# Block-causal attention and a gated MLP on one core: the MLP in 9 chunks of 512 tokens instead of 16 halves of 288

## The chip, the cores and the metric

The kernel runs on one core of one Trainium2 chip. The metric is device microseconds for one execution; the median of three runs of the kernel before is 1021.64 us (1021.4 to 1022.11). A profile of one execution of the kernel before is shown as well. PE is the matrix engine, PEld its weight loads, DVE, ACT and POOL are the vector, scalar and GpSimd engines, SP is the engine that issues most of the transfers.

## The reference

Attention over 8 batches, 8 heads, 576 tokens and 64 channels a head, where a token sees its own block of 64 and all earlier blocks. Its output, brought to tokens by 512 channels, goes through a gated MLP without a nonlinearity.

```python
scores = scale * np.matmul(q, k.transpose(0, 1, 3, 2))      # scale = 1/8
scores = np.where(block_i >= block_j, scores, -1e9)
attn = softmax(scores)                                       # max taken off, sum + 1e-09
x = np.matmul(attn, v) -> (8 * 576 tokens, 8 * 64 channels)
a = x @ w1                                                   # 512 x 1024
b = x @ w2                                                   # 512 x 1024
h = a * b @ w3                                               # 1024 x 1024
out = h @ w_out                                              # 1024 x 512
```

The kernel multiplies w3 by w_out once and keeps the product as `wh`, `wl`. There are 4608 tokens in all: 8 batches of 576, or 9 times 512.

## The kernel before

**Number format.** A factor is held as two parts, a rounded one (`..h`, `hi`) and the remainder (`..l`, `lo`), both in the matmul type `fp32r`; a product takes three matmuls, high by high, low by high, high by low. ACT or DVE writes the high part, POOL mostly the low one.

**Attention.** The work goes by pairs of heads, n = 0 to 31, four pairs to a batch. `load(n)` brings q, k and v of a pair in one transfer of 896 KB (128 partitions x 1792 numbers) into one of two buffers `raw`. For each of the two heads j of a pair, `prep_qk` makes `hi[j]` (the rounded q and k), two transfers that copy halves of it (`hi<-hi`, `lo<-hi`), and two POOL subtractions of 64x576 numbers for the remainders. `shift_mask` computes a bound of each block's row maximum with cheap matmuls, and two small transfers `lo<-ms`, one for each head, put it into a row of `lo[j]`. `prep_v` splits v into `vs` with one ACT cast and one POOL subtraction. `s_tile` then makes scores `s` in five steps S0 to S4 a head (widths 288, 288, 448, 320, 192+64), the exponentials `p` and `ph` on ACT, the remainder `pl` on DVE and the running row sum `rsum` on POOL. `pv` multiplies `ph`, `pl` by `vs` in five steps c = 0 to 4 into `x`. The first four pairs (n < 4) use plain fp32 and run while the weights are decoded.

**x.** `take` adds the two halves of `x` in PSUM into `x32`, `norm` divides by the row sum, and `finish_x` splits the pair's 576 tokens at once into two halves of 288: ACT casts `xh`, POOL subtracts `xl`. 12 such buffers of each kind exist, so the MLP of a batch reads them while the next batch's are filled.

**MLP.** `gen_moe(b)` handles a batch as two halves of 288 tokens. For each of 8 steps f it makes two sums `ab` of 12 matmuls of 288 columns; then ACT copies one (`a32`), DVE multiplies (`g32`), ACT casts `gh`, POOL subtracts `gl`. For each of 4 steps e it makes one sum `o` of 24 matmuls, which ACT copies (`o32`) and SP writes out as `out_t` (144 KB). A `yield` stands after every 6 matmuls, and such a piece is the unit of interleaving.

**What sets the order.** The table `PLAN` (one row for each head of a pair) is a list of letters: S a score step, V a pv step, B and A the prepare steps of this pair's second and the next pair's first head, M a step of the mask, Q `prep_v` of the next pair and, in the second head, `load(n + 2)`, R, N, T the sums, `take` and `norm`, and F one MLP piece. There are 24 F in the two rows, so 24 pieces a pair, 28 pairs long. From pair 4 on PE executes exactly the written order. The other engines' queues are put in order by a scheduler that works with due times. What the interleaved pieces don't cover runs at the end, with no attention beside it.

**Queues.** All transfers but those of the first pairs are issued by SP, one after the other; an issue that waits for a buffer holds those behind it. A buffer `raw` comes free for `load(n + 2)` when its last reader is done, which is the POOL subtraction of `prep_v` (`vs<-raw`). The scheduler moves loads up: `load(17)`, written in pair 15, is issued at the end of pair 14.

## Time and profile before

| what | value |
|---|---|
| median of 3 runs | 1021.64 us |
| profiled execution: span from first to last instruction | 1019.4 us |
| what lies around the span, by the median | 2.2 us |
| mean granted TensorE clock | 0.982 |
| PE busy | 965.8 us (95%) |
| DVE, ACT, POOL busy | 744.7, 547.4, 596.6 us |

The profiled execution's own device time is not listed beside its span; the span is compared with the median of the runs, which lie within 0.7 us. Three stages are seen. In the first 160 us four pairs run in plain fp32 while the weights are loaded and decoded. From about 170 to 940 us the 28 other pairs run, some 27.5 us each, with MLP pieces between their steps. From 943 to 1016.2 us only the MLP is left. Matmul records carry a duration longer than their pitch, since they overlap; so the time that a matmul costs is read from the distance between starts.

In rows of the profile a form such as `128x288` is partitions by elements, and `[0.29 <-ACT ph L252]` says how long the engine idled before the instruction and what ended it.

### The profile page before, as it was taken

The numbers are of one execution on the slowest core, as the hardware profiler recorded it, in microseconds if no ns is written. First come the engines' busy times: TensorE is split into PE (matmuls) and PEld (weight loads), VectorE is DVE, ScalarE is ACT, GpSimd is POOL, SyncE is SP. The second block draws the span as 40 slices with busy tenths as digits, with TensorE's granted clock in tenths as the row PEclk, the third lists the DMA queues.
The fourth block names the chain that finished last, engine by engine and source line by source line (L and its number), as shares of the span: only waits on it lengthen the run. The fifth ranks groups of instructions, "written<-read, shape, count | busy, mean of one in ns | idle before, by whom it ended". The sixth has DMA issues, their size and how long they took to land.

```text
span 1019.4 us, 18475 instructions
## 1 busy us (share of the span) xinstructions
PE 965.8 (95%) x6594; PEld 888.3 (87%) x6624; DVE 744.7 (73%) x1320; ACT 547.4 (54%) x1433; POOL 596.6 (59%) x625
## 2 busy tenths in 40 slices
PE   3878878999999999999999999999999999999998
PEld 1444346999999999999999999999999999999998
DVE  7899886777787777777777778777777777775100
ACT  3645555656555555555565655555555556553221
POOL 3242466667676666767576767666675757673211
PEclk9889897999999999999999999999999999999999
DMA  8566542122212222222212221222222221110000
GB/s 299 170 205 196 172 122 59 49 83 61 61 51 69 73 60 73 66 78 61 84 49 84 61 66 46 70 72 64 69 67 78 60 85 48 48 25 25 1 24 24
DMA packets 37436, 80.42 MB, mean 79 GB/s; under 512 B 5408, under 2 KB 21920, under 8 KB 37344
## 3 DMA queue, kind: packets, MB, share of 16 engines
q1 hardware_dynamic: 35564, 76.26, 24.5%
q10 hardware_dynamic: 1780, 2.97, 1.2%
q8 instruction: 52, 0.85, 0.4%
q14 instruction: 40, 0.33, 0.1%
HBM read 50.76 MB, written 9.44 MB: 59 GB/s over the span
## 4 chain that ended last, share of the span: by engine, by line
PE 67%; DVE 16%; ACT 8%; issue 4%; DMA 4%; SPq 0%; ACTq 0%; POOL 0%; DVEq 0%; POOLq 0%
PE ab L387 28%; PE o L403 20%; PE s L236 7%; PE x L291 6%; DVE pl L254 5%; PE mx L183 3%; ACT ph L252 2%; ACT p L251 2%; DVE g L394 2%; PE x L275 1%; DVE wbits L138 1%; DMA wraw<-in_w 1%; DMA wraw<-in_w3t 1%; DVE wbits L136 1%; DVE x L329 1%
## 5 line engine op out<-in xcount | busy, mean ns | idle before, releaser
L257 POOL TENSOR_TENSOR rsum<-rsum,p 128x448 f32<-128x448 f32 x224 | 176.7, 789 | 108.4 <-ACT p L251 98.6
L254 DVE TENSOR_TENSOR pl<-p,ph 128x448 fp32r<-128x448 f32 x168 | 148.3, 896 | 60.1 <-ACT ph L252 59.2
L396 POOL TENSOR_TENSOR gl<-g,gh 128x288 fp32r<-128x288 f32 x128 | 107.5, 840 | 120.1 <-ACT gh L395 118.7
L395 ACT CAST gh<-g 128x288 fp32r<-128x288 f32 x128 | 55.5, 433 | 217.1 <-DVE g L394 217.1
L387 PE MATMUL ab<-xh,w2h 128*128 128x288 f32 x512 | 154.4, 301 | 0.0
L403 PE MATMUL o<-gh,wh 128*128 128x288 f32 x512 | 153.7, 300 | 0.0
L387 PE MATMUL ab<-xh,w1h 128*128 128x288 f32 x512 | 151.7, 296 | 1.6 <-ACT xh L338 1.6
L387 PE MATMUL ab<-xl,w2h 128*128 128x288 f32 x512 | 151.8, 296 | 0.0
L387 PE MATMUL ab<-xl,w1h 128*128 128x288 f32 x512 | 151.4, 296 | 0.3 <-POOL xl L339 0.3
L387 PE MATMUL ab<-xh,w2l 128*128 128x288 f32 x512 | 151.7, 296 | 0.0
L387 PE MATMUL ab<-xh,w1l 128*128 128x288 f32 x512 | 151.4, 296 | 0.0
L403 PE MATMUL o<-gl,wh 128*128 128x288 f32 x512 | 151.1, 295 | 0.0
L403 PE MATMUL o<-gh,wl 128*128 128x288 f32 x512 | 151.0, 295 | 0.0
L187 DVE TENSOR_REDUCE m<-mx 128x1 f32<-128x512 f32 (+6 forms) x320 | 128.7, 449 | 19.3 <-PE mx L183 17.4
L252 ACT ACTIVATE ph<-s 128x288 fp32r<-128x288 f32 x336 | 131.3, 393 | 0.8 <-issue 0.8
L236 PE MATMUL s<-hi 128*128 128x288 f32 (+4 forms) x384 | 123.0, 332 | 6.8 <-ACT pe L244 4.0
L211 POOL TENSOR_TENSOR hi<-raw,hi 64x576 fp32r<-64x576 f32 x64 | 92.9, 1451 | 33.3 <-ACT hi L157 16.4
L254 DVE TENSOR_TENSOR pl<-rsum,ph 128x288 fp32r<-128x288 f32 x112 | 74.6, 685 | 49.0 <-ACT ph L252 48.8
L251 ACT ACTIVATE p<-s 128x448 f32<-128x448 f32 x224 | 85.4, 381 | 46.3 <-PE s L236 43.3
L236 PE MATMUL s<-lo 128*128 128x288 f32 (+4 forms) x384 | 106.8, 306 | 3.4 <-issue 2.5
L394 DVE TENSOR_TENSOR g<-ab,a 128x288 f32<-128x288 f32 x128 | 57.7, 451 | 71.3 <-PE ab L387 63.3
L291 PE MATMUL x<-ph,vs 128*128 128x128 f32 x336 | 104.2, 320 | 0.0
(73 smaller groups left out, 2418.1 us busy)
## 6 DMA issues: line engine op xcount, KB each, us to landing
raw<-in_qkv SPq DMA_DIRECT2D x32, 896.0 KB
out_t<-o SPq DMA_DIRECT2D x64, 144.0 KB
wraw<-in_w3t SPq DMA_DIRECT2D x16, 512.0 KB
wraw<-in_w SPq DMA_DIRECT2D x16, 512.0 KB
hi<-hi SPq DMA_DIRECT2D x54, 144.0 KB
lo<-hi SPq DMA_DIRECT2D x54, 144.0 KB
wraw<-in_wout SPq DMA_DIRECT2D x8, 512.0 KB
hi<-hi ACTq DMA_DIRECT2D x10, 144.0 KB
```

What stands on the lines that cost most here:

```text
L187: nc.vector.reduce_max(m[:, col : col + 1], sc, axis=AX.X)
L211: nc.gpsimd.tensor_tensor(out=hi[j][x, 1, :], in0=rqk[o, 1, :], in1=hi[j][o, 1, :], op=ALU.subtract)
L236: nc.tensor.matmul(t[ks, at : at + q1 - q0], src[:, 1, kr], src[:, 0, q0:q1], start=(s == 0), stop=(s == 1))
L251: nc.scalar.activation(p32, t[ks, at : at + w], AF.Exp, scale=SCALE)
L252: nc.scalar.activation(ph[ks, o : o + w], t[ks, at : at + w], AF.Exp, scale=SCALE)
L254: nc.vector.tensor_tensor(out=low, in0=p32, in1=ph[ks, o : o + w], op=ALU.subtract)
L257: nc.gpsimd.tensor_tensor(out=r, in0=r, in1=p32, op=ALU.add)
L291: nc.tensor.matmul(xps[:, to : to + w], v[:, c, :], pr[:, a : a + w], start=(u < 2 and s == 0), stop=(u in (0, len(PV) - 1) and s == len(p ...
L387: nc.tensor.matmul(t[:, 0:HALF], l[:, c, fs], r, start=(c == 0 and s == 0), stop=(c == NC - 1 and s == 2))
L394: nc.vector.tensor_tensor(out=g32, in0=acc[1][:, 0:HALF], in1=a32, op=ALU.mult)
L396: nc.gpsimd.tensor_tensor(out=gl[:, f, :], in0=g32, in1=gh[:, f, :], op=ALU.subtract)
L403: nc.tensor.matmul(t[:, 0:HALF], l[:, f, es], r[:, f, :], start=(f == 0 and s == 0), stop=(f == NF - 1 and s == 2))
```

## The change

**Tokens.** The MLP goes over all 4608 tokens in 9 chunks of 512 (`gen_moe(i)`, i = 0 to 8), so a chunk may span two batches. A matmul, an `ab` or `o` sum and the ACT, DVE and POOL instructions behind it have 512 columns. There are 9 x (192 + 96) = 2592 MLP matmuls instead of 16 x 288 = 4608. A piece is now 3 matmuls. The plan is unchanged, with 24 F a pair; the first 7 chunks are interleaved, and the last two run at the end.

**x.** `take` and `norm` work in `ring`, four fp32 buffers of 1024 tokens; a batch of 576 tokens that crosses the ring's end is written in two pieces (batches 1, 3, 5 and 7). `finish_x` is gone. In its place `split_x(i, c)` makes one buffer `xh[c]`, `xl[c]` of 512 tokens just before its chunk: three of a chunk's four splits are written behind the o steps 0 to 2 of the chunk before, the fourth at the chunk's start. For chunk 0 all four stand at its start.

**Buffers.** `a32` and `o32` share one buffer, `g32` has one, where each had two. `kb` shares a buffer with `rb`.

**Loads.** q and k of a pair (128x1152, 576 KB) and v (128x640, 320 KB) come in two transfers. `raw` still has two buffers, `rawv` has one.

What the diff doesn't show is where these instructions come to stand. On SP, at the end of pair 14, before (`raw17` is the load of pair 17, `ms15` the mask row of pair 15; 0 and 1 behind `lo` are the heads):

```order
L209 DMA hi1_85<-hi1_85 64x576
L210 DMA lo1_87<-hi1_85 64x576
L200 DMA lo0_86<-ms15_5246 1x9x64
L200 DMA lo1_87<-ms15_5246 1x9x64
L94 DMA raw17_5592<-in_qkv 128x1792
```

and in the changed kernel at the same place:

```order
L221 DMA hi1_82<-hi1_82 64x576
L222 DMA lo1_84<-hi1_82 64x576
L98 DMA raw17_4464<-in_qkv 128x1152
L212 DMA lo0_83<-ms15_4205 1x9x64
L103 DMA rawv16_4185<-in_qkv 128x640
L212 DMA lo1_84<-ms15_4205 1x9x64
L428 DMA out_t<-o32_4237 128x512
```

The load of q and k has moved from behind the two mask rows to a place before them; the load of v stands between them, and ahead of the first at the end of pairs 20 to 23, 28 and 29, as here at the end of pair 20:

```order
L221 DMA hi1_82<-hi1_82 64x576
L222 DMA lo1_84<-hi1_82 64x576
L98 DMA raw23_6132<-in_qkv 128x1152
L103 DMA rawv22_5847<-in_qkv 128x640
L212 DMA lo0_83<-ms21_5867 1x9x64
L212 DMA lo1_84<-ms21_5867 1x9x64
```

On ACT, in the first head of pair 14, steps S3 and S4, before:

```order
L251 ACTIVATE p14_0_4956<-s14_0_4953 128x320
L252 ACTIVATE ph_1147<-s14_0_4953 128x320
L395 CAST gh_1152<-g32_4976 128x288
L251 ACTIVATE p14_0_4992<-s14_0_4987 128x192
L252 ACTIVATE ph_1147<-s14_0_4987 128x192
```

and in the changed kernel:

```order
L415 CAST gh_1127<-g32_3956 128x512
L263 ACTIVATE p14_0_3978<-s14_0_3975 128x448
L264 ACTIVATE ph_1122<-s14_0_3975 128x448
L263 ACTIVATE p14_0_3986<-s14_0_3983 128x320
L264 ACTIVATE ph_1122<-s14_0_3983 128x320
L413 COPY a32_4044<-ab_3968 128x512
L263 ACTIVATE p14_0_4006<-s14_0_4001 128x192
L264 ACTIVATE ph_1122<-s14_0_4001 128x192
```

Between the exponentials of S3 and S4 stood a cast `gh`, which follows a DVE product; there stands now a copy `a32`, which follows a PE sum, and the cast has moved ahead of S2's exponentials.

On POOL, in the second head of pair 14, before:

```order
L257 TENSOR_TENSOR rsum_1148<-rsum_1148,p14_1_5125 128x320
L257 TENSOR_TENSOR rsum_1148<-rsum_1148,p14_1_5155 128x192
L257 TENSOR_TENSOR rsum_1148<-rsum_1148,p14_1_5160 64x64
L211 TENSOR_TENSOR hi1_85<-raw15_4842,hi1_85 64x576
L213 TENSOR_TENSOR lo1_87<-raw15_4842,hi1_85 64x576
L396 TENSOR_TENSOR gl_1153<-g32_5192,gh_1152 128x288
L226 TENSOR_TENSOR vs1_1151<-raw15_4842,vs1_1151 128x5x64
```

and in the changed kernel:

```order
L269 TENSOR_TENSOR rsum_1123<-rsum_1123,p14_1_4111 128x320
L359 TENSOR_TENSOR xl0_1133<-ring0_88,xh0_1129 128x512
L359 TENSOR_TENSOR xl1_1134<-ring1_89,xh1_1130 128x512
L269 TENSOR_TENSOR rsum_1123<-rsum_1123,p14_1_4131 128x192
L269 TENSOR_TENSOR rsum_1123<-rsum_1123,p14_1_4136 64x64
L223 TENSOR_TENSOR hi1_82<-raw15_3904,hi1_82 64x576
L225 TENSOR_TENSOR lo1_84<-raw15_3904,hi1_82 64x576
L416 TENSOR_TENSOR gl_1128<-g32_4164,gh_1127 128x512
L238 TENSOR_TENSOR vs1_1126<-rawv15_3902,vs1_1126 128x5x64
```

Two subtractions `xl` of 512 columns have come in ahead of S4's row sums in this pair, which is one where a chunk ends. The last reader of `raw` is now the subtraction for `lo1`, one place ahead of `gl`; `vs1` reads `rawv`.

The diff, cut where lines only hand arguments through:

```diff
-HALF = S // 2
-RAW = 2 * S + 640
+TOK = 512
+NCHUNK = NT // TOK
+RING = 2 * TOK
+QK = 2 * S
+VW = 640
...
+    ring = [cpool.tile([P, RING], F32, name=f"ring{c}") for c in range(NC)]
...
     def load(n):
-        t = raws.tile([P, RAW], F32, tag="raw", name=f"raw{n}")
-        nc.sync.dma_start(out=t, in_=qkv[n // NPAIR, n % NPAIR])
+        t = raws.tile([P, QK], F32, tag="raw", name=f"raw{n}")
+        nc.sync.dma_start(out=t, in_=qkv[n // NPAIR, n % NPAIR][:, 0:QK])
         raw_of[n] = t
 
+    def load_v(n):
+        t = raws.tile([P, VW], F32, tag="rawv", name=f"rawv{n}", bufs=1)
+        nc.sync.dma_start(out=t, in_=qkv[n // NPAIR, n % NPAIR][:, QK : QK + VW])
+        v_of[n] = t
...
-        tl["gh"] = pool.tile([P, NF, HALF], F32R, name="gh")
-        tl["gl"] = pool.tile([P, NF, HALF], F32R, name="gl")
+        tl["gh"] = pool.tile([P, NF, TOK], F32R, name="gh")
+        tl["gl"] = pool.tile([P, NF, TOK], F32R, name="gl")
+        tl["xh"] = [pool.tile([P, TOK], F32R, name=f"xh{c}") for c in range(NC)]
+        tl["xl"] = [pool.tile([P, TOK], F32R, name=f"xl{c}") for c in range(NC)]
...
-        kb = work.tile([P, S], BF16, tag="kb", name=f"kb{n}")
+        kb = work.tile([P, S], BF16, tag="tr", name=f"kb{n}")
...
+    def pieces(n):
+        at, left, done = (n // NPAIR) * S % RING, S, 0
+        while left:
+            w = min(left, RING - at)
+            yield slice(done, done + w), slice(at, at + w)
+            done, at, left = done + w, (at + w) % RING, left - w
...
-    def take(n, j, xps, x32):
+    def take(n, j, xps):
         o, x = own[j], oth[j]
-        xl = tl["late"].tile([P, S], F32, tag="xlow", name=f"xlow{n}_{j}")
-        nc.scalar.copy(xl[o], xps[x, 384:960])
-        nc.vector.tensor_tensor(out=x32[o], in0=xps[o, 384:960], in1=xl[o], op=ALU.add)
+        for a, r in pieces(n):
+            dst = ring[n % NPAIR][o, r]
+            cols = slice(384 + a.start, 384 + a.stop)
+            nc.scalar.copy(dst, xps[x, cols])
+            nc.vector.tensor_tensor(out=dst, in0=xps[o, cols], in1=dst, op=ALU.add)
...
-        (nc.gpsimd if n < 2 else nc.vector).tensor_tensor(out=x32, in0=x32, in1=rb, op=ALU.mult)
-
-    def finish_x(n, x32):
-        for h in range(2):
-            at = (2 * n + h) % 12
-            pool, bufs = (xpool, 8) if at < 8 else (tl["late"], 4)
-            xh = pool.tile([P, HALF], F32R, tag="xh", name=f"xh{n}_{h}", bufs=bufs)
-            xl = pool.tile([P, HALF], F32R, tag="xl", name=f"xl{n}_{h}", bufs=bufs)
-            src = x32[:, h * HALF : (h + 1) * HALF]
-            nc.scalar.copy(xh, src)
-            nc.gpsimd.tensor_tensor(out=xl, in0=src, in1=xh, op=ALU.subtract)
-            x_of[n // NPAIR, n % NPAIR, h] = (xh, xl)
+        for a, r in pieces(n):
+            dst = ring[n % NPAIR][:, r]
+            (nc.gpsimd if n < 2 else nc.vector).tensor_tensor(out=dst, in0=dst, in1=rb[:, a], op=ALU.mult)
+
+    def split_x(i, c):
+        src = ring[c][:, i * TOK % RING : i * TOK % RING + TOK]
+        nc.scalar.copy(tl["xh"][c], src)
+        nc.gpsimd.tensor_tensor(out=tl["xl"][c], in0=src, in1=tl["xh"][c], op=ALU.subtract)
...
+    def gen_moe(i):
+        gh, gl = tl["gh"], tl["gl"]
+        xh, xl = tl["xh"], tl["xl"]
+        for c in range(0 if i == 0 else NC - 1, NC):
+            split_x(i, c)
+        for f in range(NF):
+            fs = slice(f * P, (f + 1) * P)
+            acc = []
+            for a, b2 in ((w1h, w1l), (w2h, w2l)):
+                t = ps_m.tile([P, TOK], F32, tag="psm", name="ab")
+                for c in range(NC):
+                    for s, (l, r) in enumerate(((a, xh[c]), (b2, xh[c]), (a, xl[c]))):
+                        nc.tensor.matmul(t, l[:, c, fs], r, start=(c == 0 and s == 0), stop=(c == NC - 1 and s == 2))
+                    if c < NC - 1 or len(acc) == 0:
+                        yield
+                acc.append(t)
+            a32 = tl["late"].tile([P, TOK], F32, tag="e32", name="a32", bufs=1)
+            g32 = tl["late"].tile([P, TOK], F32, tag="g32", name="g32", bufs=1)
+            nc.scalar.copy(a32, acc[0])
+            nc.vector.tensor_tensor(out=g32, in0=acc[1], in1=a32, op=ALU.mult)
+            nc.scalar.copy(gh[:, f, :], g32)
+            nc.gpsimd.tensor_tensor(out=gl[:, f, :], in0=g32, in1=gh[:, f, :], op=ALU.subtract)
+            yield
+        for e in range(DM // P):
+            t = ps_m.tile([P, TOK], F32, tag="psm", name="o")
+            es = slice(e * P, (e + 1) * P)
             for f in range(NF):
+                for s, (l, r) in enumerate(((wh, gh), (wl, gh), (wh, gl))):
+                    nc.tensor.matmul(t, l[:, f, es], r[:, f, :], start=(f == 0 and s == 0), stop=(f == NF - 1 and s == 2))
+                if f < NF - 1:
+                    yield
+            o32 = tl["late"].tile([P, TOK], F32, tag="e32", name="o32", bufs=1)
+            nc.scalar.copy(o32, t)
+            nc.sync.dma_start(out=out_t[es, i * TOK : (i + 1) * TOK], in_=o32)
+            if e < NC - 1 and i + 1 < NCHUNK:
+                split_x(i + 1, e)
+            yield
...
                             prep_v(n + 1, j)
+                            if j == 1 and n + 2 < NN:
+                                load_v(n + 2)
                         if j == 1 and n + 2 < NN:
                             load(n + 2)
...
+    load_v(NPAIR + 1)
...
-    mlp = (None for b in range(B - 1) for _ in gen_moe(b))
+    mlp = (None for i in range(B - 1) for _ in gen_moe(i))
...
-    fill(gen_moe(B - 1), 1000)
+    for i in range(B - 1, NCHUNK):
+        fill(gen_moe(i), 1000)
```

64 lines of the change are left out of this document (17 added, 47 removed).

## The prediction

> **What bounds the kernel now.** I read the totals first, then the stages, then PE's waits, then single pairs.
>
> ```profile
> span 1019.4 us, 18475 instructions
> PE 965.8 (95%) x6594; PEld 888.3 (87%) x6624; DVE 744.7 (73%) x1320; ACT 547.4 (54%) x1433; POOL 596.6 (59%) x625
> 200.00:900.00 700.00, 695.38 (x5124) 675.37 (x5149) 544.14 (x961) 405.07 (x1117) 469.99 (x508) 1.00 0.22 65
> 943.00:1016.20 73.20, 73.19 (x552) 72.95 (x551) 7.33 (x16) 15.72 (x38) 12.89 (x16) 1.00 0.04 15
> ```
>
> The lower two rows are windows: length, then busy us and instructions of PE, PEld, DVE, ACT and POOL, then the granted clock, the DMA engines' share and GB/s. From 200 us on PE is busy 99% (695.38 of 700) at clock 1.00, and the tail is nothing but PE. So after the first 160 us the time is PE's work plus what PE waits for. Work taken from ACT, DVE or POOL is worth nothing by itself; a result that reaches PE later costs its whole delay. PE's two kinds of wait that bear on the change are these groups of the waits (us in total, times, longest):
>
> ```profile
> PEld x L291 <- DVE pl L254: 9.9, 27, 0.5
> PE s L236 <- DMA lo<-ms: 0.8, 1, 0.8
> ```
>
> The first comes back in nearly every pair. The second happened once, but shows that a mask row can hold PE.
>
> **The matmuls: −2 us.** PE's price of one is the distance between starts.
>
> ```profile
> 501.58 0.36 PE L236 MATMUL s<-hi 128*128 128x448 f32 x1
> 501.77 0.36 PE L236 MATMUL s<-lo 128*128 128x448 f32 x1
> 501.97 0.31 PE L236 MATMUL s<-hi 128*128 128x320 f32 x1
> ```
>
> 448 columns take 0.19 and 0.20 us here, 0.42 to 0.46 ns a column. In the tail window 552 matmuls of 288 columns take 73.2 us, 0.1326 each or 0.460 ns a column. So the price is close to proportional to the columns, and 512 cost 0.235 (by 0.46). 4608 x 0.1326 = 611.0 us become 2592 x 0.235 = 609.1. Bounds: with 448 columns at 0.195, 512 cost 0.223, which is 578 us in all (−33); at 0.240, 622 (+11). I take the proportional value, since 448 is the nearest width and lies between. A piece shrinks from 0.796 (6 x 0.1326) to 0.705 us, 0.091 less: 24 pieces in 28 pairs give some 61 us up, and the two chunks at the end, 576 matmuls and 135 us, take them back.
>
> The Trainium skill (TensorE: Matmul & The Clock Gate, section "Back-to-back issue gap") gives an isolated gap of N/2.4 + 2.5 ns, by which the sum would be an estimated −5 us (215.8 against 122.5 ns); the tail's 132.6 for 288 is above it. The same section gives some 131 ns at 512 in a sustained stream, which would be an estimated −270 us; the 190 to 200 ns above for 448 speak against it.
>
> **The wait for `pl`: −10 us.** First head of pair 14, around S4's scores and pv step c = 3:
>
> ```profile
> 504.65 0.25 PE L236 MATMUL s<-hi 128*128 128x192 f32 x1
> 505.54 0.46 DVE L394 TENSOR_TENSOR g<-ab,a 128x288 f32<-128x288 f32 x1
> 506.03 0.43 ACT L395 CAST gh<-g 128x288 fp32r<-128x288 f32 x1 [2.23 <-DVE g L394]
> 506.38 0.32 ACT L251 ACTIVATE p<-s 128x192 f32<-128x192 f32 x1
> 506.95 0.62 DVE L254 TENSOR_TENSOR pl<-p,ph 128x192 fp32r<-128x192 f32 x1 [0.29 <-ACT ph L252]
> 507.30 0.25 PE L291 MATMUL x<-ph,vs 128*128 128x192 f32 x1
> 507.62 0.36 PE L291 MATMUL x<-pl,vs 128*128 128x192 f32 x1
> ```
>
> S4's scores are done at about 504.9, but ACT idles 2.23 us for DVE's `g`, casts `gh`, and only then makes `p`; `pl` ends at 507.57, and PE's second matmul starts 0.32 after the first where 192 columns cost 0.09. The group of the weight loads counts it from the load's side, 9.9/27 = 0.37 a pair. In the changed order `a32` stands there, which follows PE alone, and `gh` stands ahead of S2's exponentials, where DVE is a step earlier. The wait should go in all 28 pairs: −10 (bounds −10 and 0, if `a32` is late instead).
>
> **The mask row behind the load: +21 us.** The second head of pair 14 and the start of pair 15:
>
> ```profile
> 516.99 0.25 PE L236 MATMUL s<-hi 128*128 128x192 f32 x1
> 517.52 0.33 ACT L251 ACTIVATE p<-s 128x192 f32<-128x192 f32 x1 [0.67 <-PE s L236]
> 518.00 1.03 POOL L257 TENSOR_TENSOR rsum<-rsum,p 128x192 f32<-128x192 f32 x2 [0.96 <-ACT p L251]
> 519.11 1.42 POOL L211 TENSOR_TENSOR hi<-raw,hi 64x576 fp32r<-64x576 f32 x1
> 520.60 1.43 POOL L213 TENSOR_TENSOR lo<-raw,hi 64x576 fp32r<-64x576 f32 x1
> 522.11 0.80 POOL L396 TENSOR_TENSOR gl<-g,gh 128x288 fp32r<-128x288 f32 x1
> 523.33 0.26 ACT L193 ACTIVATE ms<-mt 9x128 fp32r<-9x128 f32 x1
> 523.50 0.88 POOL L226 TENSOR_TENSOR vs<-raw,vs 128x320 fp32r<-128x320 f32 x1 [0.59 <-ACT vs L157]
> 523.62 1.58 SPq L200 DMA_DIRECT2D lo<-ms  x2
> 525.29 0.41 SPq L94 DMA_DIRECT2D raw<-in_qkv  x1
> 526.16 0.29 PE L236 MATMUL s<-lo 128*128 128x288 f32 x1
> ```
>
> Count from 516.99. POOL's second subtraction ends at +5.04 (522.03) and the mask row is ready at +6.6; its transfer is issued there, and PE reads it at +9.17 (526.16). Eight pieces stand between, each 0.091 shorter, so PE will want it at +8.44. Before, the load waited for `vs` and went behind the mask rows. Now its buffer is free at +5.04, so it is issued at +5.1, ahead of them on SP, and its data are ahead of theirs. What the load occupies:
>
> ```profile
> 526.20:527.20 1.00, 1.00 (x9) 1.00 (x9) 0.37 (x1) 0.60 (x2) 0.09 (x1) 1.00 0.81 143
> 527.20:528.20 1.00, 1.00 (x10) 1.00 (x9) 0.19 (x1) 1.00 (x5) 1.00 (x2) 1.00 0.88 366
> 528.20:529.20 1.00, 1.00 (x9) 0.99 (x9) 1.00 (x2) 0.38 (x2) 0.49 (x1) 1.00 0.89 373
> 529.20:530.20 1.00, 1.00 (x9) 0.98 (x8) 0.54 (x2) 0.80 (x3) 0.28 (x1) 1.00 0.09 36
> ```
>
> 896 KB keep the 16 engines busy 0.81 + 0.88 + 0.89 + 0.09 = 2.67 us and end some 4.0 after the issue (529.3 less 525.29). 576 KB are 0.643 of that, 0.95 less: 3.1 to 3.3 after the issue. Held behind them, the mask row lands at +8.3 to +8.6 against the +8.44 that is wanted. Three kinds of pair differ:
>
> - ten regular ones: about 0.1 each, together +1;
> - five at a chunk's end (n = 7, 11, 15, 19, 27), where two `xl` of 512 columns stand ahead of S4's row sums. POOL's 288 columns cost 0.82 and its 512 columns 1.5 in the groups below, 1.46 by the columns, so two cost 2.9; POOL's idle 0.96 and an earlier start for the first take about 1.8 of it, and 1.1 stay: 1.2 each, +6;
> - five (n = 8, 12, 16, 20, 28) where an `out_t` of 256 KB lies between, 256/896 x 2.67 = 0.76: 0.86 each, +4.3;
> - six (n = 21 to 24, 29, 30) where `rawv` goes first too. It waits for POOL's `gl` (512 columns, 1.44 by 0.80 x 512/288) and `vs` (0.88) behind +5.04, so +7.4, then 0.41 of issue and 0.95 of data: the mask row at +9.9, 1.5 each in four of them (6.0); 23 has the two `xl` as well, 1.5 + 1.1 = 2.6; in 24 an `out_t` lies in the queue, but no `gl` on POOL, 1.5 − 1.44 + 0.76 = 0.8 at the least and 1.5 at the most, 1.2: +9.8.
>
> ```profile
> L148 POOL TENSOR_TENSOR w2l<-wbits,w2h 128x512 fp32r<-128x512 f32 x8 | 11.9, 1505 | 12.8 <-ACT w2h L147 12.7
> L339 POOL TENSOR_TENSOR xl<-x,xh 128x288 fp32r<-128x288 f32 x64 | 51.1, 819 | 52.6 <-ACT xh L338 52.4
> ```
>
> That is 1 + 6 + 4.3 + 9.8 = +21. Bounds: were every landing 0.8 earlier (2.3 to 2.5 after the issue, as at the 373 GB/s of the third window with 0.8 before the first byte), 0.4 x 5 + 0.06 x 5 + 0.7 x 4 + 1.8 + 0.4 = 7 would stay; 0.5 later for each pair is 21 + 26 x 0.5 = 34. Whether a small transfer really waits for a large one no row here shows; the load fills the engines to 0.81 to 0.89 of their time, so I take that it does, and the case that it doesn't is a rival. On this the Trainium skill (DMA: Bandwidth & Descriptors, section "Two DMAs through the same engine are not ordered") says that within one queue of one engine descriptors start in order but are pipelined; by it the mask row waits for what its own engines still hold, which is the case I take.
>
> **Smaller terms: +2.6 us.**
>
> ```profile
> 511.98 0.41 ACT L252 ACTIVATE ph<-s 128x288 fp32r<-128x288 f32 x1
> 512.60 0.37 PE L236 MATMUL s<-hi 128*128 128x448 f32 x1
> 164.87 0.41 PE L387 MATMUL ab<-xh,w1h 128*128 128x288 f32 x1 [1.57 <-ACT xh L338]
> 168.41 0.74 PE L236 MATMUL s<-hi 128*128 128x448 f32 x1 [2.26 <-ACT ph L252]
> 1016.27 0.40 ACT L407 COPY o<-o 128x288 f32<-128x288 f32 x1 [2.80 <-PE o L403]
> ```
>
> S2's scores need the PSUM buffer that `ph` leaves at 512.39, 0.21 before their start; ACT's copies grow from 0.40 to about 0.7, so some heads lose a little: +1 (0 to 6, which is 0.1 for 56 heads). Where the late pairs begin PE already waited 1.57 for `xh` and 2.26 for `ph`; now all four splits of chunk 0 stand there, on ACT and POOL behind each other: +1 (0 to 2.5). At the end the last chunk's first `gl` stands behind an `xl`, and the last copy of 512 columns and its transfer are longer: +0.6. `take`'s extra pieces, `kb` in `rb`'s buffer and single `e32`, `g32` cost nothing: a step f or e spans 24 x 0.235 = 5.6 us, in which ACT has 40% free (405 of 700) and DVE 22%. Without that cover each is 0.2 to 0.5 a pair, 6 to 14 us.
>
> **Sum:** −2 − 10 + 21 + 2.6 = +11.6. The span becomes 1031.0; with the 2.2 us between the profiled span and the median, 1021.64 − 1019.4, the time is **1033 us**.
>
> **The rivals.**
>
> - *The mask row isn't held.* If the small transfer passes the load, the +21 shrink to what issue order alone costs, 0 to 7, and the gain at `pl` stands: 1021.64 − 2 − 10 + 2.6 + 0 to 7 = 1012 to 1019, middle 1016. For it: its 2 KB touch few engines, and the windows leave 11 to 19% free. Against it: the load is queued ahead of it on every engine. It decides if the wait at a head stays under about 0.35 us.
> - *Balance.* Gain and loss cancel within 0.2%: heads at about +10, the low half of their bounds. 1020 to 1024.
> - *A fixed part in each matmul.* If 512 columns cost 0.223, the matmuls give 33 and the time is near 1000. The 448-column starts at 0.19 speak for it, 288 at 0.460 a column against.
> - *DVE and POOL lengthen each other.* POOL's and DVE's instructions of 512 columns stand ahead of a `pl`, and one wait of 0.5 (the longest of the row above) comes in each of 28 pairs on top of the forecast: +14, 1047. It decides once `pl` is over 0.3 late. For it: the wait exists today; against it, DVE idles 22%. The Trainium skill (SBUF — State Buffer, section "SBUF: two separate sides") says that VectorE with two SBUF inputs and GpSimd lock a port pair for a whole instruction; by it such waits would grow with the width.
>
> That the change doesn't do what it says (a load still behind the mask rows, `gh` still ahead of S4's exponentials) is excluded by the order of instructions.
>
> **How the numbers follow.** Forecast (1026 to 1040) 0.48, mask row not held 0.24, balance 0.12, lengthening 0.10, fixed part 0.06. Differences under 0.2%, some 2 us, can't be told from no change. Slower: 0.48 + 0.10 = 0.58; same 0.12; faster 0.24 + 0.06 = 0.30. For 8 in 10 the range takes in the forecast, balance, most of the case without holding and of the lengthening: 1010 to 1047. The forecast's own range is 1026 to 1040.
>
> **What would show it.** Right: PE waits at `s<-lo` for `lo<-ms` in some 20 pairs, 0.5 to 2 us each, mostly in the pairs named; the row `x <- pl` falls from 9.9 to under 2; 512-column starts 0.235 apart; a tail of about 135 us from chunk 7 on. Wrong: no such wait at `s<-lo` (then faster), starts at 0.223, or a new wait for `pl` or `ph` as large as the mask row's. One thing the windows could not show before is what ACT's longer copies do to the first heads of the batches that cross the ring; if S0's `ph` there is late by more than 0.2, the term of +1 is too small.

## The result: 6.6% slower

The changed kernel takes 1089.24 us in the median of four runs (1087.87 to 1090.85), the kernel before 1021.88 us. The ratio is 1.0658, with a 95% interval of 1.0643 to 1.0673. The forecast was slower, but by 11.6 us instead of 67.4, and the time lies far outside the range of 1010 to 1047.

The page of the changed kernel's profile, its totals, and two windows (length, busy us and instructions of PE, PEld, DVE, ACT and POOL, granted clock, DMA share, GB/s):

```profile
span 1089.1 us, 14331 instructions
PE 980.1 (90%) x4578; PEld 765.7 (70%) x4608; DVE 747.6 (69%) x1312; ACT 538.8 (49%) x1297; POOL 596.9 (55%) x541
```
```profile
200.00:900.00 700.00, 641.30 (x3229) 523.72 (x3253) 533.75 (x939) 380.60 (x970) 453.07 (x423) 0.99 0.23 63
949.00:1085.00 136.00, 136.00 (x584) 109.42 (x583) 12.46 (x19) 26.99 (x45) 26.88 (x21) 1.00 0.04 16
```

The second window is the tail: 584 matmuls of 512 columns in 136.0 us, 0.233 each, as forecast (0.235). The first is the stage of the pairs: PE is busy 641 of 700 us, where it was 695. DVE, ACT and POOL are each less busy in this window too, and over the whole run their totals are within 9 us of those before. So most of the time isn't in anybody's work; it is in PE's waits. The groups that bear on it (us in total, times, longest; a wait may be seen on the weight load, PEld, and on the matmul behind it):

```profile
PE s L248 <- ACT ph L264: 18.7, 20, 1.1
PE s L248 <- issue: 13.3, 10, 2.5
PE s L248 <- DMA lo<-ms: 10.3, 13, 2.2
PE s L248 <- POOL xl L359: 9.8, 5, 2.3
PE mt L203 <- DVE m L201: 4.5, 8, 1.2
```

Before, these were, in the same order, 2.3, 3.0, 0.8, 0 and 1.4 us. Since a wait can be put down to the wrong releaser, the table below goes by place and not by releaser: for each place of a pair, the distance between the starts of two matmuls beyond 0.46 ns a column, worked out from the starts in each trace and summed over the pairs from 4 on.

| kernel | us | s<-lo (head of a pair) | S2 | pv c = 3 | mask's transpose |
|---|---|---|---|---|---|
| before | 1021.9 | 5.3 | 2.6 | 10.7 | 2.1 |
| changed | 1089.2 | 43.3 | 22.4 | 10.3 | 6.9 |
| difference | +67.4 | +38.0 | +19.8 | −0.4 | +4.8 |

These four places make +62. Of the 2.6 us at S2 before, 2.5 are a single wait where the late pairs begin, so S2 inside the pairs went from nothing to 22. At that beginning PE's first MLP matmuls now wait 5.19 us for `xh` and 2.21 for `xl`, instead of 1.57 and 0.34: +5.5.

Two more terms stand at no place of a pair. The matmuls themselves got cheaper: 2592 x 0.233 = 604 us instead of 611, −7. And the granted clock fell to half six times between 387 and 900 us, 3.4 us each time, which the mean of 0.99 above hides. One of these stretches and the time behind it, and two matmuls of 512 columns in it:

```profile
838.30:841.50 3.20, 3.20 (x10) 2.61 (x9) 0.92 (x2) 1.36 (x4) 0.00 (x0) 0.50 0.21 82
841.70:844.70 3.00, 3.00 (x18) 2.57 (x17) 1.63 (x2) 2.23 (x5) 1.94 (x2) 1.00 0.00 0
```
```profile
838.75 0.63 PE L407 MATMUL ab<-xh,w1h 128*128 128x512 f32 x1
839.17 0.63 PE L407 MATMUL ab<-xh,w1l 128*128 128x512 f32 x1
```

The two start 0.42 us apart instead of 0.233. In these stretches, 20.5 us in all, PE so does 55% of its work, and some 9 us are lost, though PE counts as busy. Each stretch begins during one of the longest waits for the mask row (2.0 to 2.6 us) or within 1.5 us of its end; four other waits of that length had none, and no wait under 2.0 us had one. The kernel before has no such stretch between 174 us and its last matmul. So a long wait can cost more than its length.

Together that is 62 + 5.5 − 7 + 9 = +69.5, where the two profiled spans differ by 69.7, so nearly all of the difference has a place. The rest of this document asks what made the waits at these places.

### The profile page after: what moved, and what is told of

The parts are those of the page before. It is cut to its first block, busy times and chain, and to the rows that moved or that the text cites. A ratio compares the mean times of both kernels' runs of the same rounds, so it can differ in the third digit from the quotient of the medians.

```text
span 1089.1 us, 14331 instructions
## 1 busy us (share of the span) xinstructions
PE 980.1 (90%) x4578; PEld 765.7 (70%) x4608; DVE 747.6 (69%) x1312; ACT 538.8 (49%) x1297; POOL 596.9 (55%) x541
## 4 chain that ended last, share of the span: by engine, by line
PE 52%; DVE 25%; ACT 9%; issue 7%; DMA 6%; POOL 1%; SPq 0%; ACTq 0%; DVEq 0%; POOLq 0%
PE ab L407 22%; PE o L423 14%; PE s L248 7%; DVE pl L266 6%; PE x L303 4%; DVE hi L169 3%; DVE m L199 3%; DMA lo<-ms 3%; DVE ph L266 3%; PE mx L195 2%; DVE part L321 2%; ACT ring L342 2%; PE w L383 2%; ACT ph L264 2%; DVE g L414 2%
## 5 line engine op out<-in xcount | busy, mean ns | idle before, releaser
L416 POOL TENSOR_TENSOR gl<-g,gh 128x512 fp32r<-128x512 f32 x72 | 92.6, 1286 | 191.6 <-ACT gh L415 182.4
L248 PE MATMUL s<-hi 128*128 128x288 f32 (+4 forms) x384 | 128.6, 345 | 24.1 <-ACT ph L264 18.7
L407 PE MATMUL ab<-xh,w1h 128*128 128x512 f32 x288 | 119.3, 414 | 5.2 <-ACT xh L358 5.2
L407 PE MATMUL ab<-xl,w1h 128*128 128x512 f32 x288 | 116.2, 403 | 2.2 <-POOL xl L359 2.2
L423 PE MATMUL o<-gh,wh 128*128 128x512 f32 x288 | 116.6, 405 | 0.0
L407 PE MATMUL ab<-xh,w1l 128*128 128x512 f32 x288 | 116.2, 404 | 0.0
L407 PE MATMUL ab<-xh,w2h 128*128 128x512 f32 x288 | 115.0, 399 | 0.0
L407 PE MATMUL ab<-xl,w2h 128*128 128x512 f32 x288 | 114.4, 397 | 0.0
L407 PE MATMUL ab<-xh,w2l 128*128 128x512 f32 x288 | 114.3, 397 | 0.0
L423 PE MATMUL o<-gl,wh 128*128 128x512 f32 x288 | 114.0, 396 | 0.0
L423 PE MATMUL o<-gh,wl 128*128 128x512 f32 x288 | 113.7, 395 | 0.0
```

Of the source, the lines that this page charges most:

```text
L248: nc.tensor.matmul(t[ks, at : at + q1 - q0], src[:, 1, kr], src[:, 0, q0:q1], start=(s == 0), stop=(s == 1))
L407: nc.tensor.matmul(t, l[:, c, fs], r, start=(c == 0 and s == 0), stop=(c == NC - 1 and s == 2))
L416: nc.gpsimd.tensor_tensor(out=gl[:, f, :], in0=g32, in1=gh[:, f, :], op=ALU.subtract)
L423: nc.tensor.matmul(t, l[:, f, es], r[:, f, :], start=(f == 0 and s == 0), stop=(f == NF - 1 and s == 2))
```

## Experiments

Unless an interval is given, a kernel was profiled and timed once, beside a run of the kernel before on the same chip (1022.1 to 1024.5 us); differences under some 3 us are not read.

### 1. The load behind the mask row

One head of a pair in the changed kernel, PE and SP's queue by the timeline:

```profile
543.77 0.25 PE L248 MATMUL s<-hi 128*128 128x192 f32 x1
552.01 0.29 PE L248 MATMUL s<-hi 128*128 128x288 f32 x1
552.75 0.37 PE L248 MATMUL s<-lo 128*128 128x288 f32 x1 [0.44 <-DMA lo<-ms]
```
```profile
548.85 0.34 SPq L98 DMA_DIRECT2D raw<-in_qkv  x1
550.40 0.79 SPq L212 DMA_DIRECT2D lo<-ms  x1
```

Counted from 543.77 as in the prediction, the load goes out at +5.08, the mask row at +6.63, and PE, which could have gone on at +8.37, reads it at +8.98. Both landing times, worked out from the completions in the trace, are +8.69 and +8.84: the row lands right behind the load. The experiment makes the old buffers of q, k and v come free after the first scores of the pair, so that SP issues the loads behind the mask rows:

```diff
@@ s_tile, behind the score matmuls
+        if n >= EARLY and j == 0 and todo[0][0] == 0 and todo[0][3] == 0:
+            scr = work.tile([1, 1], F32, tag="scr", name=f"scr{n}")
+            nc.vector.tensor_tensor(out=scr, in0=t[0:1, 0:1], in1=raw_of[n][0:1, 0:1], op=ALU.add)
+            if n > EARLY:
+                nc.vector.tensor_tensor(out=scr, in0=t[0:1, 0:1], in1=v_of[n][0:1, 0:1], op=ALU.add)
+                if n + 1 < NN:
+                    load_v(n + 1)
@@ pair, step Q
-                            if j == 1 and n + 2 < NN:
+                            if j == 1 and n + 2 < NN and n < EARLY:
                                 load_v(n + 2)
```

> The changed kernel, except that both loads (q and k, and v) go out only after the mask rows: two added DVE instructions of one element in a pair's first score step read the old buffers again, so that these come free later, and the load of v is written there. Theory (the mask row lands behind the load): the waits of PE at s<-lo in the changed kernel sum to 38 us; with the row issued at +6.6 and landing 1.8 later, as in the kernel before, at +8.4 against the +8.37 at which PE wants it, 0.1 to 0.2 stay in each of 27 pairs. So 1089 - 33 = 1056 us, 1050 to 1062. Rival (the row itself is late, by ACT or DVE): the waits stay, 1080 to 1090.

Measured: 1051.84 us, 37 us less. The same head of a pair in this kernel, SP and PE:

```profile
535.32 1.56 SPq L212 DMA_DIRECT2D lo<-ms  x2
537.96 0.35 SPq L98 DMA_DIRECT2D raw<-in_qkv  x1
```
```profile
528.69 0.25 PE L248 MATMUL s<-hi 128*128 128x192 f32 x1
536.98 0.29 PE L248 MATMUL s<-hi 128*128 128x288 f32 x1
537.28 0.37 PE L248 MATMUL s<-lo 128*128 128x288 f32 x1
```

The row goes out at the same +6.63, nothing stands before it, and PE waits 0.17 us instead of 0.60 (0.30 between the starts, of which 0.13 is the matmul). The place s<-lo falls from 43.3 to 11.7 us. The clock stays at 1.00 in the whole stage. S2 falls too, from 22.4 to 13.1 us, and c = 3 rises from 10.3 to 14.0. So more than half of the loss was the order of two transfers on one queue, with what followed from it. In the kernel before, the same split of the load alone:

```diff
-        t = raws.tile([P, RAW], F32, tag="raw", name=f"raw{n}")
-        nc.sync.dma_start(out=t, in_=qkv[n // NPAIR, n % NPAIR])
+        t = raws.tile([P, 2 * S], F32, tag="raw", name=f"raw{n}")
+        nc.sync.dma_start(out=t, in_=qkv[n // NPAIR, n % NPAIR][:, 0 : 2 * S])
...
+    def load_v(n):
+        t = raws.tile([P, 640], F32, tag="rawv", name=f"rawv{n}", bufs=1)
+        nc.sync.dma_start(out=t, in_=qkv[n // NPAIR, n % NPAIR][:, 2 * S : RAW])
```

> The kernel before, with halves of 288, but with q and k loaded apart from v as in the changed kernel. Theory: the load goes ahead of the mask row and lands at +8.7 there too, the row at +8.9 to +9.0, but PE wants it at +9.12 to +9.19; so nothing to 0.1 us in the pairs without an out_t, and 0.5 to 0.8 in some 13 pairs where an out_t is issued between: 1022 + 8 = 1030 us, 1023 to 1037. Rival (the split of the load alone makes the 38 us): 1050 or more. Rival (it costs nothing): 1020 to 1023.

Measured: 1027.6 us beside 1024.37, with the wait that was foretold:

```profile
PE s L243 <- DMA lo<-ms: 5.9, 14, 0.6
```

s<-lo rises from 5.3 to 13.4 us there, but the time only by 3. The load goes ahead of the row as in the changed kernel, but the load of v never does; with pieces of 0.796 us PE wants the row 0.75 us later (+9.12 to +9.19), and an `out_t` is 144 KB instead of 256. So by this comparison the order alone costs 8 us at this place, and the other 30 come from it together with the shorter pieces, the larger outputs, the splits at a chunk's end and the loads of v ahead of the row.

### 2. S2 of the second head

The other large term, in the changed kernel. First DVE, then POOL, ACT and PE:

```profile
533.88 1.34 DVE L266 TENSOR_TENSOR ph<-p,ph 64x64 fp32r<-64x64 f32 x1
535.25 0.69 DVE L199 TENSOR_REDUCE m<-mx 128x1 f32<-128x512 f32 x1
535.86 0.77 DVE L321 TRANSPOSE_TENSOR_REDUCE part<-rsum 128x18 f32<-128x576 f32 x1
536.55 0.65 DVE L414 TENSOR_TENSOR g<-ab,a 128x512 f32<-128x512 f32 x1
```
```profile
533.71 1.43 POOL L223 TENSOR_TENSOR hi<-raw,hi 64x576 fp32r<-64x576 f32 x1
```
```profile
537.24 0.62 ACT L415 CAST gh<-g 128x512 fp32r<-128x512 f32 x1 [4.44 <-DVE g L414]
537.76 0.46 ACT L169 CAST vs<-rawv 128x320 fp32r<-128x320 f32 x1
538.24 0.64 ACT L342 COPY ring<-x 64x576 f32<-64x576 f32 x1
538.90 0.41 ACT L263 ACTIVATE rsum<-s 128x288 f32<-128x288 f32 x1
539.21 0.41 ACT L264 ACTIVATE ph<-s 128x288 fp32r<-128x288 f32 x1
```
```profile
536.60 0.29 PE L248 MATMUL s<-lo 128*128 128x288 f32 x1
539.67 0.47 PE L248 MATMUL s<-hi 128*128 128x448 f32 x1 [1.13 <-ACT ph L264]
```

S2's scores need the PSUM buffer of S0, which ACT leaves at 539.62. ACT waited for DVE's `g`, made `gh`, a cast and a copy, and only then S0's exponentials; S0's scores had been there since about 536.9. Against the kernel before, counted from S0's second matmul (510.62 and 536.60), `g` starts at −0.05 instead of −0.92, and both `g` and `gh` are 0.2 longer.

What makes `g` late here can be read by comparing heads of the same kernel. The first row above is DVE's subtraction of 64x64, which takes 1.34 us while POOL's `hi<-raw` runs beside it. Where the two don't meet, it takes 0.23. In the changed kernel they meet in 22 of the 28 first heads. In 19 of these an f step ends there: `g` starts at −0.06, behind the longer subtraction and the row sum `part`, and S2 waits 0.84 to 1.28 us, 21.4 in all. In the two heads where an f step ends there and they don't meet, `g` starts at −0.89 and S2 waits 0.05 and 0.37. With the late loads of the first experiment they meet in 9 heads instead of 22, and with that S2 fell there: eight of them hold 9.3 of the 13.1 us. In the kernel before they never meet. No run takes this meeting away and leaves the row sum where it is. Four ideas were tried on S2.

**The phase of the f steps.** In the changed kernel, `DELAY = 10` instead of 3 (f steps have 8 pieces, so they end one piece earlier):

> The changed kernel with the MLP begun 10 pieces late instead of 3 (DELAY), which moves the ends of all f steps one piece earlier in every pair. Theory (PE's wait of 1.1 at S2 of each second head comes from DVE's product g and ACT's cast gh, which stand ahead of S0's exponentials and are late): g can start 0.7 us earlier and ahead of DVE's row sum, so these 20 waits of about 1.1 lose most, to under 0.4 each: 1089 - 15 = 1074 us, 1066 to 1080. Rival (ACT and DVE simply have too much with 512 columns): the same time is lost at another wait, 1085 to 1093.

Measured: 1109.68 us, 20 us more. S2 stays at 22 us, 4.2 of them in one wait where the late pairs begin; the transpose rises to 11.3 and a wait for `part` appears, 15.8 us. With the loads behind the mask rows:

> Both edits at once, loads after the mask rows and the MLP begun 10 pieces late. Theory: the two losses lie at different places of a pair and add, 1089 - 33 - 15 = 1041 us, 1033 to 1050. Rival: one wait takes the place of the other, above 1055.

Measured: 1079.24 us, 27 more than with the loads alone. The two edits don't add, and this phase is worse.

**DVE's order.** On the kernel with the late loads, the row sum `part` of the first head behind `g`:

```diff
-    "B F B F S F S B F F S S F F F S M M V F V V V F R F F V Q N",
+    "B F B F S F S B F F S S F F F S M M V F V V V F F F R V Q N",
@@ sums
+        if j == 0 and "g" in tl:
+            g = tl["g"][0:1, 0:1]
+            nc.vector.tensor_tensor(out=part[0:1, j, 0:1], in0=g, in1=g, op=ALU.add)
@@ gen_moe, behind the copy a32
+            tl["g"] = g32
```

> The kernel with the loads after the mask rows, and in each first head DVE's row-sum reduction (part) put behind the product g of the f step that ends there, by one added DVE instruction of one element that reads g. Theory (S2 of the second head waits because g is late on DVE and gh stands ahead of S0's exponentials on ACT): g starts 0.6 us earlier, so the 13 us of waits at S2 fall to some 6, 1051.8 - 7 = 1045 us, 1041 to 1049. Rival (ACT itself is too full there, g doesn't matter): the 13 us stay, 1050 to 1054.

Measured: 1050.14 us. `g` starts 0.66 us earlier and the waits of 1.25 fall to 0.6 as foretold, but behind f steps S2 keeps 9.0 of 13.0 us, other heads give back some, and the time moves by less than the single runs resolve. With the row sum out of the way `g` starts at −0.76 in the heads where DVE and POOL meet and at −0.82 to −0.90 in the others, so it takes both, the long subtraction and the row sum behind it, to make `g` as late as it was.

**POOL's width.** On the late loads, POOL subtracts only 64 columns of each `gl`; the other 448 stay zero, so the low part of the gate's product is left out there:

```diff
-            nc.gpsimd.tensor_tensor(out=gl[:, f, :], in0=g32, in1=gh[:, f, :], op=ALU.subtract)
+            nc.gpsimd.tensor_tensor(out=gl[:, f, 0:64], in0=g32[:, 0:64], in1=gh[:, f, 0:64], op=ALU.subtract)
```

> The kernel with the loads after the mask rows, but POOL subtracts only 64 of the 512 columns of each gl; the other 448 columns of gl stay zero, so the low part of the gate's product is left out of the output there. Theory (POOL's gl of 1.3 us pushes its row sums and remainders onto DVE's small instructions, and DVE is late with pl and g for it): the waits at pl and at S2, 14 and 13 us, fall by half or more, 1051.8 - 15 = 1037 us, 1030 to 1044. Rival (POOL's length doesn't matter to PE): 1048 to 1053.

Measured: 1053.86 us, no gain. The waits did move: c = 3 falls from 14.0 to 9.6 us and S2 rises from 13.1 to 17.7, with DVE's long subtraction in 15 first heads instead of 9. So the width of `gl` isn't what costs the time; this says nothing of POOL's `hi<-raw`, which is as long as before.

**The splits of x.** On the late loads, each split held until its o step is copied out:

```diff
+                nc.scalar.copy(xh[e][0:1, 0:1], o32[0:1, 0:1])
                 split_x(i + 1, e)
```

> The kernel with the loads after the mask rows, and each split of x for the next chunk held until the o step it is written behind has been copied out (one added ACT instruction of one element), so that the splits come one by one, 5.6 us apart, instead of two at once ahead of S4's exponentials. Theory (those two casts on ACT and two subtractions on POOL make the waits at pv c = 3 of the second head, 8.0 us in 7 pairs, at the mask's transpose, 4.9 us, and at S3, 2 us, in the pairs where a chunk ends): 10 to 14 of the 15 us go and some 3 come back where the splits stand now, 1051.8 - 9 = 1043 us, 1038 to 1047. Rival (the same work waits elsewhere): 1049 to 1054.

Measured: 1045.01 us, 7 less. c = 3 falls from 14.0 to 9.7 and the transpose from 6.7 to 2.7; S2 rises from 13.1 to 16.7. Two splits at once ahead of S4 were a cause. Late row sum and late splits together:

> The edits of the late row sum and of the late splits together, on the loads after the mask rows. Theory: they lie at different places and add, 1051.8 - 16 = 1036 us, 1031 to 1043. Rival (one wait takes the other's place): 1043 or more.

Measured: 1039.85 us, the best that was reached with chunks of 512, still 16.5 us above the kernel before in that job (1023.33). S2 holds 12.4 us, s<-lo 10.6, c = 3 8.8. Four edits on top of it went for these:

```diff
@@ e8: the 64x64 remainder of first heads on POOL
+            (nc.gpsimd if c == 4 and j == 0 else nc.vector).tensor_tensor(out=low, in0=p32, ...)
@@ e9: and DVE's cast of hi behind pl of S4
+            low = tl["pl"][0:1, PC[3] : PC[3] + 1]
+            nc.vector.tensor_tensor(out=hi[j][0:1, 0, 0:1], in0=low, in1=low, op=ALU.add)
         cast(n, hi[j][o], rqk[o], CAST[0])
@@ e10 (without e8, e9): the first head's copy of x and cast of vs behind S0's exponentials of the second
+            nc.scalar.copy(dst[0:1, 0:1], after)      # after = ph[0:1, 0:1]
             nc.scalar.copy(dst, xps[x, cols])
@@ e11: and the second head's behind the mask row, the transpose ahead of the row-sum matmul
-    "M A S S A F F S F M M S F F F S M A M V V V F V F F V N Q F R T M F F",
+    "M A S S A F F S F M M S F F F S M A M V V V F V F F V F R M N Q T F F",
```

> The kernel with late loads, late row sum and late splits (1039.9 us), and the subtraction of the 64x64 remainder (ph<-p,ph) of each first head moved from DVE to POOL. Theory (DVE spends 1.33 us there because POOL's 1.42 us subtraction hi<-raw runs beside it, where the same instruction cost 0.23 to 0.5 alone, and this makes g late): DVE reaches g a microsecond earlier, and the 9.3 us of waits at S2 behind f steps fall to 3: 1034 us, 1031 to 1037. Rival (POOL doesn't hold DVE; g waits for PE's sum): 1038 to 1042.

Measured: 1048.85 us, S2 16.8. DVE's small subtraction costs 0.32 on POOL, but now `g` waits for PE's own sum:

```profile
335.89 0.69 DVE L425 TENSOR_TENSOR g<-ab,a 128x512 f32<-128x512 f32 x1 [1.34 <-PE ab L417]
```

So with the row sum out of the way `g` is as early as PE lets it be, and some 0.53 us stay at S2 of this head: `g` starts 0.09 later than in the kernel before, `g` and `gh` are 0.23 and 0.19 longer, and PE asks 0.18 earlier (two pieces); less the slack of 0.21 that is 0.48. Half of the 9 us that the whole lost has a place. The one-element instruction that holds the row sum back takes 0.7 to 0.9 us in ten first heads and 3.05 in one, beside POOL's subtractions, where it took 0.15 to 0.71 before. S0's exponentials overwrite `rsum` and start 0.09 us behind the row sum there, so S2 goes from 12.4 to 16.8. The rest isn't settled.

> The same with DVE's cast hi<-raw of the next pair (1.15 us) held behind pl of S4 in each first head, by one added DVE instruction of one element. Theory (the cast stands ahead of that pl and makes the 0.35 to 0.6 us of wait at pv c = 3 of the first head): 8.8 us there fall to 4 on top of the edit before, 1029 us, 1026 to 1034. Rival (what waits is p on ACT, not pl on DVE): no gain over the edit before.

Measured: 1103.09 us. c = 3 falls to 0.7 as foretold, but S2 takes 54.8. That isn't the cast, since `g` starts as early as in the run before. It is the one-element instruction again:

```profile
345.08 3.36 DVE L332 TENSOR_TENSOR part<-g 1x1 f32<-1x1 f32 x1
349.42 0.41 ACT L273 ACTIVATE rsum<-s 128x288 f32<-128x288 f32 x1 [2.69 <-DVE part L334]
```

In 16 first heads it takes 3.0 to 3.4 us, through three POOL subtractions in a row, and the row sum and S0's exponentials come that much later. Behind 13 of these waits the clock falls to half, 44 us in all. So this time tells of the way in which the order was made, not of the order.

> The kernel with late loads, late row sum and late splits (1039.9 us), with ACT's copy of the first head's x into the ring and its cast of vs held behind S0's exponentials of the second head, by one added ACT instruction of one element before each. Theory (what is left of the S2 waits, 9.3 us behind f steps and 3.1 behind o steps, is ACT reaching S0's exponentials late: gh is 0.19 wider, g 0.2, the two pieces of work ahead cost 1.1): S2 waits fall to 2, 1040 - 10 = 1030 us, 1026 to 1035. Rival (another resource of S2, or the x buffer coming free later, takes its place): 1037 or more.

Measured: 1069.65 us. S2 falls to 4.9 as foretold; s<-lo rises to 20.1, the transpose to 11.4, and the row sum makes a wait of its own:

```profile
PE tot L337 <- DVE part L333: 6.5, 18, 0.5
```

> The same, with the second head's copy of x and cast of vs on ACT held behind the mask row ms, and the mask's transpose before the row-sum matmul on PE. Theory (the 10.6 us left at s<-lo are ACT making the row 0.1 to 0.7 us late behind that copy): the row is ready 0.6 us earlier, s<-lo waits fall to 3, 1030 - 7 = 1023 us, 1018 to 1029. Rival (DVE's maxima set the row): 1028 or more.

Measured: 1073.38 us. s<-lo falls to 5.2 as foretold, the transpose takes 24.1:

```profile
PE mt L203 <- DVE m L201: 21.0, 26, 1.3
```

In the last two the wait that was aimed at went, and the time went up all the same: a step of a queue was moved past another that PE needs as well.

### 3. Does the relief at c = 3 exist?

The prediction counted 10 us there. In the changed kernel the wait of the first head did go (from 0.49 to 0.16 us between the two starts, median of 28), yet S2 grew. In the kernel before this can be done alone: the cast `gh` and `gl` of a step are written two pieces later, and one ACT instruction of one element puts `gh` behind S4's exponentials.

```diff
@@ gen_moe: gh and gl of step f are written by tick(), two pieces later
+            if tl.get("hold") is not None:
+                nc.scalar.copy(gh[0:1, f, 0:1], tl["hold"])
             nc.scalar.copy(gh[:, f, :], g32)
             nc.gpsimd.tensor_tensor(out=gl[:, f, :], in0=g32, in1=gh[:, f, :], op=ALU.subtract)
@@ pair, from S4 of the first head to its row sum
+                            tl["hold"] = tl["ph"][0:1, PC[3] + 128 : PC[3] + 129]
```

> The kernel before, with the cast gh that stands between S3's and S4's exponentials of each first head held behind S4's (the cast and its gl are written two pieces later, and one added ACT instruction of one element orders them). Theory 1 (the relief at pv c = 3 is real): the 28 waits of 0.37 us for pl go and nothing comes in their place, 1022 - 10 = 1012 us, 1010 to 1015. Theory 2 (the relief comes back: with p 1.2 us earlier POOL's subtraction hi<-raw falls on DVE's ph<-p,ph, so g and S0's exponentials of the second head are late, as in the changed kernel): new waits at S2 of 0.3 to 0.8 us a pair, 1020 to 1033.

Measured: 1024.25 us beside 1022.63, no gain. The waits of this kernel:

```profile
PE s L236 <- ACT ph L252: 7.3, 27, 2.3
PEld x L291 <- DVE pl L254: 1.7, 7, 0.3
```

c = 3 falls from 10.7 to 1.9, and S2 rises from 2.6 to 11.8, 0.35 us a pair. The way back is in the trace, first the kernel before, then this one:

```profile
507.60 0.50 DVE L254 TENSOR_TENSOR ph<-p,ph 64x64 fp32r<-64x64 f32 x1
509.70 0.46 DVE L394 TENSOR_TENSOR g<-ab,a 128x288 f32<-128x288 f32 x1 [0.19 <-PE ab L387]
```
```profile
509.88 1.43 POOL L211 TENSOR_TENSOR hi<-raw,hi 64x576 fp32r<-64x576 f32 x1
510.05 1.34 DVE L254 TENSOR_TENSOR ph<-p,ph 64x64 fp32r<-64x64 f32 x1
512.72 0.42 DVE L410 TENSOR_TENSOR g<-ab,a 128x288 f32<-128x288 f32 x1
```

With `p` earlier, DVE's subtraction of 64x64 falls on POOL's `hi<-raw`. They meet in 26 of the 28 first heads, where they never met before; in these 26 `g` starts at −0.35 instead of −0.92 and S2 waits 0.33 to 0.39 us, in the other two not at all. That is the second theory above. So the relief is real, and it comes back 5 us later in the same pair. The term of −10 was no gain at this phase of the f steps, with 288 columns either.

The same kernel with the f steps one piece earlier or later (`DELAY = 2` and `DELAY = 4` instead of 3):

> The kernel before with the MLP begun 2 pieces late instead of 3, so every f step ends one piece (0.8 us) earlier against the pair. Theory (the phase of the f steps against the pair decides which exponentials stand behind a cast that waits for DVE): the time changes by 5 us or more either way, and the waits at c = 3 and S2 change with it. Rival (the phase doesn't matter with steps of 3.2 us): within 3 us of 1022.

Measured: 1012.6 us, and again in rounds:

> The kernel before with DELAY 2, again, timed in rounds. Theory: 1012.6 us is the phase and comes again, ratio 0.990 to 0.992. Rival (chance of one run): 0.995 or more.

Measured: 1013.45 us, ratio 0.9918 (0.9896 to 0.9940). This beats both kernels. c = 3 has 1.7 us and S2 2.0, and in the window from 200 to 900 us PE has no idle time left:

```profile
200.00:900.00 700.00, 700.00 (x5189) 682.93 (x5214) 535.65 (x977) 408.85 (x1128) 494.51 (x514) 1.00 0.23 66
```

> The same, 4 pieces late, every f step ends one piece later. Theory: a change of 5 us or more either way, the other way than with 2 pieces if the place of the cast against S4 decides. Rival: within 3 us of 1022.

Measured: 1099.07 us. Here the queue of SP shows the first experiment's cause again, in the kernel before and with the whole load of 896 KB:

```profile
560.30 0.34 SPq L94 DMA_DIRECT2D raw<-in_qkv  x1
560.73 1.57 SPq L200 DMA_DIRECT2D lo<-ms  x2
```
```profile
PE s L236 <- DMA lo<-ms: 24.9, 8, 3.8
```

In every other pair the buffer comes free before the row is made, the load goes out first, and PE waits about 3.5 us; s<-lo takes 52.2 us, 47 more. Twelve of these 13 waits are followed by half clock, 68 us in all, in which the distances between the matmuls' starts show some 26 us lost. The two make 73 of the 76 us.

Last, the changed kernel with late loads and late splits at two more phases:

> The changed kernel with late loads and late splits (1045 us), the MLP begun 6 pieces late. f steps then end at pieces 6, 14 and 22 of a pair, which are places where they end without a wait in the kernel before with 2 pieces. Theory (phase): the waits at S2, 14 us, and at c = 3, 10 us, lose most, 1020 to 1032. Rival (512 columns as such): 1040 or more.

Measured: 1043.29 us. S2 falls to 4.0, all of it one wait where the late pairs begin, but c = 3 takes 14.9 and the transpose 14.6.

> The same, 5 pieces late: ends at pieces 5, 13 and 21. Theory (phase): another time than with 3 and 6 pieces, by 5 us or more, with other waits. Rival (512 columns as such): 1040 to 1050.

Measured: 1062.71 us, with c = 3 at 22.7, the transpose at 15.9 and s<-lo at 19.1.

So phase moves the changed kernel too, by 20 us between these two; but of the four phases tried with the late loads, one of them without the late splits, none came under 1043 without the late row sum. With chunks of 512 an f step spans 8 pieces, and each of its instructions on DVE, ACT and POOL is a longer block in a queue; that this is why no phase fits is argued, not shown. Four of the eight phases weren't tried.

## Why the prediction was wrong, point by point

- **The matmuls, −2.** Near enough: 0.233 a matmul in the tail instead of 0.235 makes −7, inside the bounds, and the two chunks there take 576 x 0.233 = 134 us.
- **The clock, no term at all.** The sum took the clock of 1.00 of the pairs as given. Six stretches at half clock behind long waits for the mask row cost some 9 us.
- **The mask row behind the load, +21, bounds 7 to 34.** The mechanism was right, the size too small: +38.0, above the upper bound. The steps up to the issue were right to 0.1 us (load at +5.1, row made at +6.6, wanted at +8.44 against 8.37; the rows called pair 14 in the prediction are by their time those of pair 16, which changes no number). The failed step is "3.1 to 3.3 after the issue" for the landing of 576 KB: it took 3.6. For the regular ten that made 0.5 to 1.0 each (one 1.5) instead of 0.1; where an `out_t` lies between, the row landed at +10.3 and the wait was 1.9 to 2.1 instead of 0.86; with `rawv` ahead the row landed at +10.9 instead of +9.9, 2.4 to 2.6 instead of 1.2 to 2.6. The 4.0 from which it started, the end of the engines' work on 896 KB, isn't the landing: the completions in that trace come 4.7 after the issue. The 0.95 taken off for the smaller size was near the 1.1 that was measured. The 0.8 before the first byte in its lower bound was 0.97 here. The five pairs at a chunk's end were below their 1.2 (0.7 to 0.9), but lost 0.6 more at the transpose, which wasn't on the list.
- **S2, +1, bounds 0 to 6.** The worst step: +19.8. It was sized by the growth of one ACT copy against a slack of 0.21 us. What ends the wait is a chain, `g` on DVE, `gh` on ACT, two more ACT instructions, S0's exponentials, and it was not followed. DVE's subtraction, lengthened from 0.23 to 1.33 beside POOL, and the row sum behind it put `g` 0.83 late in 19 heads, an estimated 16 us; the longer `g` and `gh` and the shorter pieces make most of the rest. The prediction's last paragraph names a late `ph` as what would show the term too small, but for the batches that cross the ring; it came wherever an f step ends at the end of a first head.
- **The wait for `pl`, −10.** It went in the first heads, as worked out, and then wasn't a gain. The kernel before with only that wait taken away is no faster: DVE's subtraction then falls on POOL's, and the wait comes back at S2. In the changed kernel the second heads also got a new wait at c = 3 from two splits at once, so that the place shows −0.4.
- **The smaller terms.** At the start of the late pairs PE's waits for `xh`, `xl` and `ph` went from 4.2 to 7.4 us, +3 instead of +1.
- **The rivals.** "The mask row isn't held" is refuted by the first experiment. "Lengthening" came, but not as it was described: not at `pl` and not by the width of the new instructions, but between two instructions that both kernels have, brought together by the new order. Balance didn't come, and of the fixed part in the pitch only the 5 us above the forecast's −2. None of the rivals, nor the range, allowed several terms to be wrong the same way: the bounds of the heads and of S2 alone would have reached 1033 + 13 + 5 = 1051, and the −10 not coming 1061.

The Trainium skill (DMA: Bandwidth & Descriptors, section "Two DMAs through the same engine are not ordered") says that descriptors of one queue on one engine start in order; the row that lands 0.15 us behind a load issued 1.5 us before it agrees, and with nothing ahead of it the row takes 1.8 us.

## What to carry to other kernels

A buffer that comes free earlier lets its load start earlier, and on an in-order queue that load then stands in front of whatever small transfer the critical engine waits for; look at what is issued behind it, and price it with landing times of whole transfers, not with engine time alone. Before a wait is counted as a gain, follow the instruction that it frees to the next queue with little slack, or take away that wait alone in the old kernel. Where a fixed table interleaves two streams, try the phase of one against the other first: one number moved this kernel from 1021.6 to 1013.5 us one way and to 1099 the other. And look at the granted clock behind each long wait of PE: the mean of a stage hid a loss of 9 us here and of 26 us there. An instruction that is added only to keep an order can be held up itself; look at its length before the result is read.
